# Eight x loads issued from ScalarE's queue in place of SyncE's in a fused state-space and mixer kernel

## The chip, the cores and the metric

The kernel runs on one core of one Trainium2 chip. The metric is the device time of one execution in microseconds. Three runs of the kernel before gave 232.43 us in the median (231.18 to 232.94).

The engines are named as in the profile: PE is TensorE, PEld its weight loads, DVE is VectorE, ACT is ScalarE, POOL is GpSimd, and SP is SyncE, which here issues DMAs and does nothing else. "SPq" in a profile line is SP's sequencer at work on an issue.

## The reference

Two blocks, one after the other, in float32. The first is a state-space block with decay, for 4 batches, 8 heads, 768 positions, head dimension 32 and state size 16, in chunks of positions:

```
cum = np.cumsum(log_a[chunk])                     # a clipped to [1e-6, 1]
M   = (C @ B.T) * exp(cum_i - cum_j) * causal
y   = M @ x + (C @ state) * exp(cum)
state = exp(sum(log_a)) * state + (B * exp(cum_last - cum)).T @ x
```

Its result, with the heads side by side as 256 columns, is `x` of the second block, a mixer:

```
h  = x.T @ U @ V                                  # over positions, rank 32
u  = x + h.T
out = u + relu(u @ w_ch1) @ w_ch2                 # 256 -> 1024 -> 256
```

U, V and the two w arrive as 64-bit floats and are turned into float32 on the chip, from their words.

## The kernel before, in words

**Tiling.** The 768 positions of a batch are three pairs of two blocks of 128; there are twelve pairs in all, numbered 0 to 11. For each pair there are five loads: `x` in two halves of 128 KB (`load_x`, lines 203 to 210), and B in two halves and C in one (`load_bc`, lines 188 to 201), which fill one `bc` tile. Tiles of `x` and of `bc` have four buffers each.

**Order.** The kernel is recorded under a manual schedule. Two strings of words give the whole order: `LOADS` (line 34) ahead of the constants, and `PLAN` (line 36) behind them. A word is a letter and numbers: `b2.0` is part 0 of the bc load of pair 2, `x2.0` is half 0 of its x load, `Z0` the four loads of V, `z0` the load of U, `W0` or `w5` a weight load, `c0` the next step in the conversion of a loaded weight. Each engine executes its instructions in the order in which the words record them. The words around the loads in question are

```
    'b0.0 b0.1 b0.2 x0.0 x0.1 b1.0 b1.1 b1.2 ')
    'b3.2 F1.1 F1.0 x1.1 x1.0 A0 Q0.1 Q0.0 Z0 A1 Q0.2 V0.1.1 V0.0.0 K0 s0 g0 m0 M0 n0 ...
    ... z0 c0 x2.1 c0 V2.1.3 n1 i1 c0 g2 m2 j1 y1 x2.0 s2 u2 ...
    ... j2 c1 y2 m3 x3.1 t1 O2.1 x3.0 c2 p0 b4.1 P4 s3 v0 ...
```

Behind `LOADS` stand the constants and the logarithm of the decays: the load of `a`, two transposes (line 329), a clip on VectorE, and `la` on ScalarE (line 335).

**The words.** `A0` and `A1` (`decays`) compute the decay factors `F`: products on TensorE, then an exponential on ScalarE (line 372). `Q` and `P` (`prep`) multiply the loaded B and C by `F` into `BC` on VectorE. `V` and `T` (`turn`) transpose `BC` on TensorE and copy the result to `T` and `Cm` on ScalarE or VectorE. `g` (`gram`, line 509) and `m`, `M` (`mask`) form the masked products of C and B. `s` (`state`, line 541) multiplies `BC` by `x`, and needs both halves of `x`; `u` (`update`) carries the state on, on VectorE. `n` (`intra`, line 633) multiplies the masked products by `x`; `i` and `j` (`inter`, line 611) add what comes from the state. `y` (`yout`, line 646) copies the result to `yT` on ScalarE. `t` and `O` transpose it to `ytok` (lines 654 and 663). `p`, `q`, `v`, `a` are the low-rank product of the mixer, `U`, `d`, `S`, `f`, `e`, `h` its two large products (line 726). `F` words are warm-up products on the identity (line 137).

**Queues.** All loads go through `begin` (line 183), which issues them from SP; results are stored from SP too (line 795). A load finished is told by a semaphore. There are eight of them for loads, given out in turn in the order of all loads, so that every load from the ninth on waits until the load eight places before it, on the same semaphore, has landed. A load into a buffer in use waits for the engine that reads it last. An instruction that waits holds up those behind it on its engine.

Of the kernel before, what the change touches and what calls it, by code (L numbers as in the profile page):

```python
# [13 lines left out]
FP32R = mybir.dt.float32r  # L14
WCOLS = 512
NWORDS = 15
PLAIN = 2
TAGS = {(2, 1): "yyy", (3, 0): "yyy", (3, 1): "yyy"}

# [56 lines left out]
def kernel(  # L76
# [27 lines left out]
    nc = tc.nc  # L104
# [42 lines left out]
    class Kept:  # L147
# [23 lines left out]
        out=a_sb,  # L171
# [3 lines left out]
    x_sb, bc_sb = {}, {}  # L175
    pairs = [(b, q) for b in range(NB) for q in range(NPR)]

    def hold(load, until):

        tc.add_manual_dep(load.ins, until.ins.name, mybir.DependencyInfo(  # L180
            mybir.DependencyClass.Sync, mybir.DependencyReason.DATA))

    def begin(**kwargs):
        op = nc.sync.dma_start(**kwargs)  # L184
        if until:
            hold(op, until.pop())

    def load_bc(k, parts=(0, 1, 2)):
        b, q = pairs[k]
        if k not in bc_sb:  # L190
            bc_sb[k] = raw.tile([P, NH, 2, 2, N], FP32, tag="bc", name="bc")
        for part in parts:
            if part == 1:
                begin(
                    out=bc_sb[k][:, :, 1].rearrange("p h t n -> p h (t n)"),
                    in_=C[b, :, ts(q, 2 * P), :].rearrange("h (p t) n -> p h (t n)", t=2))
            else:
                c = part // 2
                begin(
                    out=bc_sb[k][:, :, 0, c],  # L200
                    in_=B[b, :, ts(2 * q + c, P), :].rearrange("h s n -> s h n"))

    def load_x(k, blocks=(0, 1)):
        b, q = pairs[k]
        if k not in x_sb:
            x_sb[k] = raw.tile([P, 2, NH, D], FP32, tag="x", name="x")
        for c in blocks:
            begin(
                out=x_sb[k][:, c],
                in_=x[b, :, ts(2 * q + c, P), :].rearrange("h s d -> s h d"))  # L210


# [17 lines left out]
    def words_of(dst):  # L230
        p, i, j = dst.shape
        t = raw.tile([P, 2 * WCOLS], INT32, tag="words", name="words", bufs=NWORDS)
        weights.append((dst, t[:p, :2 * i * j]))
# [42 lines left out]
    def load(k):  # L276
        if k < NB * NPR:
            load_bc(k)
            load_x(k)

    loads = dict(B=load_bc, X=load_x, w=load_w, b=lambda k, p: load_bc(k, (p,)),
                 x=lambda k, c: load_x(k, (c,)), W=load_w, Z=lambda n: load_v(),
                 z=lambda n: load_u())
    for word in LOADS.split():
# [43 lines left out]
    for g in range(2):  # L328
# [3 lines left out]
        out=la.rearrange("p b c h -> p b h c"),  # L332
# [64 lines left out]
    def to_fp32(dst, words, n):  # L397
# [5 lines left out]
        def tmps(*dtypes):  # L403
            t = raw.tile([P, 2 * WCOLS], INT32, tag="words", name="words", bufs=NWORDS)
            return [t[:p, v * WCOLS:v * WCOLS + i * j].bitcast(d) for v, d in enumerate(dtypes)]
# [23 lines left out]
    def refine(c):  # L429
# [6 lines left out]
        yield  # L436
        far = raw.tile([P, 2 * WCOLS], INT32, tag="words", name="words", bufs=NWORDS).bitcast(
            FP32)[:, :WCOLS].rearrange("p (i j) -> p i j", i=near.shape[1])
# [232 lines left out]
    def mixer(b):  # L671
# [61 lines left out]
        def pair(dtype):  # L733
            t = raw.tile([P, 2 * WCOLS], INT32, tag="words", name="words", bufs=NWORDS)
            return t.bitcast(dtype)[:, :2 * HS].rearrange("p (m t) -> p m t", m=2)
# [35 lines left out]
        def down(j, k, n):  # L771

            parts = b or j >= PLAIN
            pieces = 6 if parts else 4
# [130 lines left out]
```

## Time and profile before

| | |
|---|---|
| median of three runs | 232.43 us |
| the profiled execution | 231.95 us |
| span of its profile | 230.2 us |
| TensorE busy | 219.4 us (95%) |
| VectorE busy | 158.5 us (69%) |
| ScalarE busy | 113.2 us (49%) |
| GpSimd busy | 14.3 us (6%) |
| x loads | 24, 128.0 KB each, 4.0 us from issue to landing in the median |
| chain that ended last | PE 82%, DVE 7%, DMA 5%, ACT 2%, issue 2%, SPq 1% |

The profile is of one execution. Its slices divide the span into forty; a digit is the busy share of an engine in tenths, and PEclk is the clock granted to TensorE in tenths of the full one. Timeline lines give start and duration in us, engine, line of the kernel, operation, output and input, shape and count, and in brackets how long the engine was idle just before and what ended that. Lines of the chain give start, duration and what ran or was waited for. A line of the DMA view gives destination and source, the issuing engine, the number of issues, KB of each and the median time from issue to landing. A line of busy time by stretch gives the stretch, its length, TensorE's busy time with the number of products, the granted clock, the share of the DMA engines and GB/s.

### The profile page before, as it was taken

Reading aid. Unit: us, or ns where it says so; the run is one execution under the profiler, and the core shown is the slowest. Engines: PE = TensorE matmul, PEld = TensorE weight load, DVE = VectorE, ACT = ScalarE, POOL = GpSimd, SP = SyncE. Lnnn points to the kernel's source line nnn. Section 1 sums busy time; section 2 is a strip of 40 time slices with the busy share of each in tenths; the row PEclk is TensorE's granted clock in tenths of the full one; section 3 lists DMA queues with packets and bytes.
Section 4 is the critical chain, followed back from the end, with each engine's and each line's share of the span. In section 5 each row is a group of like instructions: output and inputs, shape, how many; then the busy total and the mean of one; then the engine's idle time right before and its main releaser. Section 6 shows DMA issues by size and latency. Waiting matters only on the chain.

```text
span 230.2 us, 6970 instructions
## 1 busy us (share of the span) xinstructions
PE 219.4 (95%) x2994; PEld 182.6 (79%) x2994; DVE 158.5 (69%) x331; ACT 113.2 (49%) x260; POOL 14.3 (6%) x37
## 2 busy tenths in 40 slices
PE   7698899999999999999999999999999999999993
PEld 5444656656677898898799899798998899999993
DVE  4656879989998667657964766668725983765821
ACT  3334447866976247343523553466326526655510
POOL 3011201003100000110210000010000000000000
PEclk9977999999999999999999999999999999999999
DMA  6968796898826170001001035000001001000011
GB/s 90 117 98 146 129 228 146 248 164 157 114 34 89 29 111 23 23 4 48 3 7 41 1 62 107 21 3 1 3 23 48 0 0 48 6 17 26 24 46 46
DMA packets 69518, 14.56 MB, mean 63 GB/s; under 512 B 63792, under 2 KB 67696, under 8 KB 69488
## 3 DMA queue, kind: packets, MB, share of 16 engines
q1 hardware_dynamic: 69488, 14.13, 33.0%
q8 instruction: 23, 0.38, 0.7%
q14 instruction: 7, 0.06, 0.1%
HBM read 10.98 MB, written 3.15 MB: 61 GB/s over the span
## 4 chain that ended last, share of the span: by engine, by line
PE 82%; DVE 7%; DMA 5%; ACT 2%; issue 2%; SPq 1%; POOL 0%; DVEq 0%; ACTq 0%
PE x L726 28%; PE z L726 21%; PE y L726 12%; PE y L611 3%; PE y L633 3%; DMA x<-in_x_dram 3%; PE w L680 2%; PE x L509 2%; PE w L478 2%; PE w L654 2%; PE w L541 2%; DMA bc<-in_B_dram 2%; DVE S L158 1%; DVE words L158 1%; SPq L184 1%
## 5 line engine op out<-in xcount | busy, mean ns | idle before, releaser
L158 DVE SCALAR_TENSOR_TENSOR words<-words 128x768 fp32r<-128x768 f32 (+6 forms) x44 | 35.0, 814 | 1.1
L726 PE MATMUL x<-u,w 128*128 128x384 f32 x144 | 33.2, 350 | 0.0
L726 PE MATMUL z<-u,w 128*128 128x384 f32 x144 | 32.5, 344 | 0.0
L731 ACT ACTIVATE x<-x 128x384 f32<-128x384 f32 (+1 forms) x30 | 13.6, 454 | 29.7 <-PE x L726 29.6
L726 PEld LDWEIGHTS x<-u,w 128*128 128x128 f32 x144 | 24.2, 188 | 2.3 <-DVE words L158 0.8
L158 DVE SCALAR_TENSOR_TENSOR words<-x,words 128x384 fp32r<-128x384 f32 x24 | 13.3, 556 | 17.7 <-ACT words L760 16.9
L726 PEld LDWEIGHTS z<-u,w 128*128 128x128 f32 x144 | 24.4, 188 | 0.8 <-ACT z L731 0.4
L726 PE MATMUL x<-w2c,words 128*128 128x256 f32 x112 | 22.5, 341 | 0.0
L726 PEld LDWEIGHTS x<-w2c,words 128*128 128x128 f32 x112 | 18.2, 189 | 1.8 <-DVE w2c L158 0.3
L726 PE MATMUL y<-w,words 128*128 128x256 f32 x144 | 19.5, 282 | 0.0
L726 PEld LDWEIGHTS y<-w,words 128*128 128x128 f32 x144 | 18.7, 188 | 0.2
L731 ACT ACTIVATE z<-z 128x384 f32<-128x384 f32 (+1 forms) x27 | 12.5, 462 | 12.3 <-PE z L726 11.8
L158 DVE SCALAR_TENSOR_TENSOR words<-z,words 128x384 fp32r<-128x384 f32 x24 | 13.2, 550 | 3.3 <-ACT words L760 3.3
L760 ACT ACTIVATE words<-z 128x384 fp32r<-128x384 f32 x24 | 11.4, 490 | 6.7 <-PE z L726 6.7
L158 DVE SCALAR_TENSOR_TENSOR S<-S,kept,w 128x64 f32<-128x64 f32 x40 | 11.2, 279 | 4.3 <-PE w L541 2.4
L760 ACT ACTIVATE words<-x 128x384 fp32r<-128x384 f32 x24 | 11.5, 490 | 4.7 <-PE x L726 4.6
L567 POOL TENSOR_TENSOR Sm<-S,own 128x256 f32<-128x256 f32 (+1 forms) x12 | 8.9, 738 | 80.0 <-DVE S L158 74.9
L611 PE MATMUL y<-T,Sm 32*64 32x64 f32 x352 | 12.4, 240 | 1.2 <-POOL settled L574 0.9
L726 PE MATMUL x<-w,words 128*128 128x256 f32 x96 | 13.4, 287 | 0.0
L611 PEld LDWEIGHTS y<-T,Sm 32*64 32x64 f32 x352 | 8.7, 131 | 4.9 <-issue 2.0
L633 PEld LDWEIGHTS y<-M,x 64*32 64x32 f32 x768 | 8.9, 107 | 4.5 <-DVE M L158 1.2
L726 PEld LDWEIGHTS x<-w,words 128*128 128x128 f32 x96 | 12.1, 189 | 0.4
(147 smaller groups left out, 401.8 us busy)
## 6 DMA issues: line engine op xcount, KB each, us to landing
words<-in_moe_w_ch_dram SPq DMA_DIRECT2D x7, 512.0 KB, 6.5
x<-in_x_dram SPq DMA_DIRECT2D x24, 128.0 KB, 4.0
out_dram<-ytok SPq DMA_DIRECT2D x24, 128.0 KB, 1.7
bc<-in_B_dram SPq DMA_DIRECT2D x24, 64.0 KB, 3.6
bc<-in_C_dram SPq DMA_DIRECT2D x12, 128.0 KB, 3.4
words<-in_moe_w_ch_dram SPq DMA_DIRECT2D x2, 256.0 KB, 3.8
words<-in_moe_V_dram SPq DMA_DIRECT2D x4, 48.0 KB, 3.9
words<-in_moe_U_dram SPq DMA_DIRECT2D x1, 192.0 KB, 4.0
```

Of the source, the lines that this page charges most:

```text
L158: self.last = call(*args, **kwargs)
L478: nc.tensor.transpose(out=tp[:, i, v], in_=s["BC"][:, i, c + v].rearrange("p h n -> p (h n)"), identity=ident)
L509: nc.tensor.matmul(out=g[r][cols, c], lhsT=s["T"][rows, 0, c, cols], rhs=s["Cm"][rows, :, :, ts(2 * c + p, Q)].rearrange("r v t i -> r v i ...
L541: nc.tensor.matmul(out=s["A"][p][ts(r, Q), v], lhsT=s["BC"][half, 0, v, 2 * r:2 * r + 2].rearrange("p h n -> p (h n)"), rhs=x_sb[k][half, ...
L567: nc.gpsimd.tensor_tensor(out=s["Sm"][:, sl], in0=s["S"][:, sl].rearrange("p i (s d) -> p i s d", s=2), in1=own2[:, b, 4 * q + sl.start:4 ...
L611: product = nc.tensor.matmul(out=y[p][ts(r % 2, H), r // 2, c], lhsT=own[ts(r, Q)], rhs=s["T"][ts(r, Q), 1, :, ts(2 * c + p, Q)].rearrange ...
L633: product = nc.tensor.matmul(out=y[p][ts(i, Q), n, c], lhsT=x_sb[k][half, c, h], rhs=s["M"][half, h // 2, c, h % 2], start=fresh(k, p, [i] ...
L654: nc.tensor.transpose(out=t[:, c, g], in_=yT[b][:, g, ts(2 * q + c, P)], identity=ident)
L680: nc.tensor.matmul(out=p[ts(c % 4, Q)], lhsT=U_sb[:, c], rhs=ytok[b][:, c], start=c < 4, stop=True, skip_group_check=True)
L726: nc.tensor.matmul(out=t, lhsT=lhsT, rhs=rhs, start=start, stop=True, skip_group_check=True)
L731: nc.scalar.activation(t, t, AF.Copy, scale=1.0 + EPS)
L760: nc.scalar.activation(gs[j, m // 2][0][:, m % 2], t, AF.Relu, scale=NEAR)
```

## The change

`begin` takes the queue as an argument, SP's unless another is given. `load_x` gives it ScalarE's for pairs 0 to 3 (`k < OWN`), which are eight loads: x0.0, x0.1, x1.1, x1.0, x2.1, x2.0, x3.1 and x3.0. Neither `LOADS` nor `PLAN` changes. The loads of pairs 4 to 11, and all other loads and stores, stay on SP. The lines of the kernel behind the new constant move down by one, so that line 541 of before is line 542 of after.

```diff
+OWN = 4
...
-    def begin(**kwargs):
-        op = nc.sync.dma_start(**kwargs)
+    def begin(queue=nc.sync, **kwargs):
+        op = queue.dma_start(**kwargs)
         if until:
             hold(op, until.pop())
...
         for c in blocks:
             begin(
-                out=x_sb[k][:, c],
+                queue=nc.scalar if k < OWN else nc.sync, out=x_sb[k][:, c],
                 in_=x[b, :, ts(2 * q + c, P), :].rearrange("h s d -> s h d"))
```

## The prediction

> **What bounds the kernel now.** I read the slices first, then the chain of work that ended last, then the timelines of ScalarE, SP and TensorE around the moved loads. The slices (each a fortieth, 5.76 us):
>
> ```profile
> PE   7698899999999999999999999999999999999993
> ...
> PEclk9977999999999999999999999999999999999999
> DMA  6968796898826170001001035000001001000011
> ```
>
> TensorE is the bound, but its first five slices (to 29 us) have holes, and there the DMA engines are as full as anywhere. Busy time by stretch says the same: TensorE is busy for 28.22 of the first 34.10 us and for 151.16 of the last 155.20. The loads of the change lie among the holes; behind them little idle TensorE time is left that could take a delay back. The chain begins:
>
> ```profile
> 2.36 3.55 DMA bc<-in_B_dram
> ...
> 6.00 0.10 DVE BC L158
> ```
>
> The start hangs on a bc load of pair 0 until 6.00. From there to 39 us the chain goes through VectorE, TensorE and ScalarE by turns, with no x load in it: the x loads of pairs 0 to 3 are early. ScalarE, start and duration:
>
> ```profile
> 4.09 0.36 ACT L335 ACTIVATE la<-la 128x192 f32<-128x192 f32 x1 [2.00 <-DVE la L158]
> 5.36 0.34 ACT L372 ACTIVATE F<-w 128x192 f32<-128x192 f32 x1 [0.91 <-PE w L365]
> ...
> 24.45 0.65 ACT L646 COPY yT<-y 128x256 f32<-128x256 f32 x2 [1.19 <-PE y L611]
> ...
> 29.99 0.65 ACT L646 COPY yT<-y 128x256 f32<-128x256 f32 x2 [0.47 <-PE y L611]
> ```
>
> SP, with the first two x pairs and the V loads that matter below:
>
> ```profile
> 3.00 1.55 SPq L184 DMA_DIRECT2D x<-in_x_dram  x2
> ...
> 7.83 1.67 SPq L184 DMA_DIRECT2D x<-in_x_dram  x2
> 9.54 2.55 SPq L184 DMA_DIRECT2D words<-in_moe_V_dram  x4
> ```
>
> The same view has x of pair 2 at 15.58 (2.15) and of pair 3 at 22.89 (4.12). SP runs ahead of the work by much: TensorE takes up these two pairs at
>
> ```profile
> 24.31 0.43 PE L541 MATMUL w<-x,BC 64*32 64x64 f32 x24
> ...
> 32.74 0.32 PE L541 MATMUL w<-x,BC 64*32 64x64 f32 x8
> 33.27 0.43 PE L541 MATMUL w<-x,BC 64*32 64x64 f32 x24 [0.22 <-ACT pT L683]
> ```
>
> **The change, part by part.** Eight issues leave SP (1.55 + 1.67 + 2.15 + 4.12 = 9.49 us of its time) and stand in ScalarE's stream where the plan names them. No compute instruction changes its place on any engine. What changes is which work stands ahead of a load, and what a waiting load holds up. The changed program's order on ScalarE begins:
>
> ```
> 3 L336 Activation la<-la 128x192 [waits DVE_49]
> 4 L185 DMACopy x<-in_x_dram 128x8x32 [waits DMAHW3_49]
> 5 L185 DMACopy x<-in_x_dram 128x8x32 [waits DMAHW5_49]
> 6 L373 Activation F<-w 128x96x2 [waits PE_49] x2
> ```
>
> *Pair 0* waits for nothing and stands behind the table load (0.81 to 2.09). Two issues of 0.78 (half of 1.55) end by 3.7, ahead of la at 4.09: nothing. If they took longer, la would move by the excess, behind the larger wait that follows.
>
> *Pair 1* is the large term. Loads take eight completion semaphores in turn, and each waits for the load before it on its own. For x1.1 that is now the second V load, for x1.0 the fourth. On SP such a wait held up loads alone; on ScalarE it stands ahead of F, which everything needs. When does the fourth V load land? SP starts them at 9.54; without the two x pairs ahead (1.59 and 1.71 with their gaps) it starts at 6.24, and the fourth is issued three quarters of 2.55 later, at 8.15. The DMA view gives the time from issue to landing of these four, and of x4.0, issued to a quiet queue at 37.90:
>
> ```profile
> words<-in_moe_V_dram SPq DMA_DIRECT2D x4, 48.0 KB, 3.9
> ...
> x<-in_x_dram SPq DMA_DIRECT2D x1, 128.0 KB, 2.6
> ```
>
> 8.15 + 3.9 = 12.05. The traffic agrees: the last bc load ahead of the V loads is issued at 7.0 and lands 4.1 later, at 11.1, behind the same data. Then x1.0 is issued (0.78), and F starts at 12.9 in place of 5.36, 7.5 later. Of this 0.3 is covered: BC waits for its bc load until 6.00 though F ends at 5.70. **+7.2.** The ends: landing after 2.1 (the a load, into empty queues) gives +5.4; V landing no sooner than now (9.54 + 1.91 + 3.9 = 15.35) gives +10.5. Queued behind the wait are F on ScalarE, then BC on VectorE and the transposes on TensorE, so all engines shift together. x1 itself is issued by 12.9 and needed at 15.12 + 7.2: hidden.
>
> *Pair 2* (in the times of now; the shift is on both sides). x2.1 stands between two conversions of the U/V words (20.94, 21.38); its 0.78 fits into the 0.89 that ScalarE then idles ahead of 22.89; without that cover it costs 0.78. x2.0 stands behind the yT copies of pair 1, which end at 25.10, while the products need it at 24.31. Issue at 25.15, landing 2.6 later: TensorE takes it up at 27.8. **+3.5.** It takes work in order, and VectorE's state update (24.93) and BC behind it wait as well. With 4.7 us to landing (the median of the x loads before 52 us) it is +5.6; with the shortest of any bc load (2.3) +3.2. I take 2.6, since SP, rid of eight issues, should have its weight loads down by then.
>
> *Pair 3.* x3.1 is issued behind the yT copies of pair 2 (end 30.64), 0.5 of issue (0.99 for the quiet pair at 37.90), then the ytok copy (0.59), then x3.0 at 31.8. Landing at 34.4, against products whose last 24 start at 33.27 behind the first 8 (some 0.1): **+1.3.** With 4.7 it is +3.4; with 2.3, +1.0. The pT copy at 32.85 keeps its time, since ScalarE idles 1.38 ahead of it.
>
> *The eight issues off SP* bring bc and weight loads forward. VectorE's waits for bc after 6.00 are one of 0.54, off the chain; TensorE's one wait for an x load is 0.2. Nothing to gain, at most 0.7.
>
> *Clock.* Busy time by stretch shows half clock in windows of 3.4 us behind stretches of thin work:
>
> ```profile
> 11.80:15.20 3.40, 3.31 (x44) 0.50 0.51 73
> ```
>
> The window ahead of it has TensorE busy for 2.35 of 3.40 and full clock. Idling through 7.2 us can put the work now at 6 to 11.8 (about 2.4 us of TensorE on the chain) at half clock: up to +2.4; if the two half-clock windows of now then fall elsewhere, the warm products of 1.29 in each become 0.65: -1.3. I take the middle, **+0.5**. The Trainium skill, in "TensorE: Matmul & The Clock Gate", Part 1: The HAM clock gate, has the clock halved after one idle window of about 3.4 us; by that rule the upper end holds here, and the sum would be 1.9 higher. The row agrees in the length of its window.
>
> **Sum:** 7.2 + 3.5 + 1.3 + 0.5 = 12.5. The profiled execution took 231.95 us (span 230.2 and 1.7 around it), 0.5 under the median of 232.43. 231.95 + 12.5 = **244.5**.
>
> **The rivals.**
>
> 1. *The first stall alone.* While F waits, loads get ahead, and x2 and x3 might come in time. Against: both are named behind copies of the pair before, whatever the shift. 231.95 + 7.2 + 0.5 = 239.6.
>
> 2. *The late loads share the engines with the weights.* ScalarE's x2.0 and x3.0 then meet 512 KB loads: 4.7 to landing. For it: DMA digits of 7 to 9 until 58 us. 7.2 + 5.6 + 3.4 + 0.5 = 16.7: 248.7. With V late as well, 252.
>
> 3. *Faster: issuing binds.* SP's row is solid with issues up to 34 us; relieved, it brings each load earlier, and the waits for loads behind the start go: 0.3 ahead of BC, 0.54 and 0.2: 1.0, so 230.9. It decides if no ScalarE instruction is held, that is if the fourth V load lands before la ends at 4.45; that SP issues it at 11.45 now speaks against it. The Trainium skill, in "Perfetto Trace Analysis", DMA Optimizations, advises this very balancing when descriptor generation is the bottleneck; the chain, with SP in it for 1%, does not bear it out here.
>
> 4. *It does nothing:* ScalarE issues its loads past its waits, and the x loads are early enough: 232. Against: SP's own issues keep their order in every row.
>
> **How the numbers follow.** Forecast 0.62, rival 1 0.14, rival 2 0.19, rival 3 0.03, rival 4 0.02. The range is 239.5 to 250.0: below lie rivals 3 and 4, above the far end of rival 2 (V and x both late). About 1% is what a measurement of this kernel can tell from no change; slower by over 1% is 0.95, within it 0.03, faster 0.02 (rival 3 in part falls within).
>
> **What would show it.** In the changed profile F starts near 13, with ScalarE idle ahead of it and the V words as releaser; then waits of TensorE for x ahead of line 542, one near 32 us (some 3.5), one near 43 (some 1.3), and the chain with x loads in it there. From 46 us on everything should be the old profile, shifted. Wrong would be F near 6; TensorE without those two waits; or a tail that is not shifted, work having been caught up.

## The result and the profile after

The changed kernel takes 243.26 us in the median of four runs (242.08 to 244.36), the kernel before beside it 231.81 (230.31 to 232.94). The ratio is 1.050, with a 95% interval of 1.042 to 1.058: slower by 11.5 us, where 12.5 were forecast. The profiled execution took 243.45 us, with a span of 241.7 in place of 230.2: 11.5 by the profile too.

The slices of the changed kernel's page (a fortieth is now 6.04 us), its chain by engine, and its x loads on ScalarE:

```profile
PE   7077859798999999999999999999999999999994
...
PEclk9659967999999999999999999999999999999998
DMA  9898912088776516100100005300001001000011
...
PE 77%; DMA 10%; DVE 5%; SPq 4%; issue 2%; ACT 1%; ACTq 0%; POOL 0%; DVEq 0%
...
x<-in_x_dram ACTq DMA_DIRECT2D x8, 128.0 KB, 3.4
```

The zero in TensorE's row is new, and so is the 5 in the sixth slice. Behind the tenth slice the row is as full as before. DMA has 10% of the chain in place of 5%. ScalarE's timeline in the changed kernel shows where the zero comes from:

```profile
0.80 1.28 ACT L167 ACT_TABLE_LOAD   x1 [0.80 <-PEq L890]
0.84 1.10 ACTq L185 DMA_DIRECT2D x<-in_x_dram  x2
4.40 0.36 ACT L336 ACTIVATE la<-la 128x192 f32<-128x192 f32 x1 [2.32 <-DVE la L159]
11.64 1.01 ACTq L185 DMA_DIRECT2D x<-in_x_dram  x2
12.70 0.56 ACT L373 ACTIVATE F<-w 128x192 f32<-128x192 f32 x2 [7.93 <-DMA words<-in_moe_V_dram]
...
29.89 0.37 ACT L647 COPY yT<-y 128x256 f32<-128x256 f32 x1 [1.58 <-PE y L612]
29.90 0.37 ACTq L185 DMA_DIRECT2D x<-in_x_dram  x1
30.16 0.38 ACT L647 COPY yT<-y 128x256 f32<-128x256 f32 x1
...
40.20 0.59 ACT L664 COPY ytok<-w 128x512 f32<-128x512 f32 x1
40.21 0.45 ACTq L185 DMA_DIRECT2D x<-in_x_dram  x1
```

ScalarE idles 7.93 us ahead of F, until V has landed; the x loads of pair 1, which come ahead of F, are issued at 11.64. F starts at 12.70 in place of 5.36. By the trace x1.1 is issued when the second V load has landed (11.62), and x1.0 at 12.06, when the fourth has (12.01). The chain of the changed kernel has that wait, on the second V load, and two more, of which the kernel before has none:

```profile
8.24 3.38 DMA words<-in_moe_V_dram
...
29.90 2.85 DMA x<-in_x_dram
...
40.21 2.92 DMA x<-in_x_dram
```

And TensorE's timeline has the waits that answer to them, ahead of the state products of pairs 2 and 3:

```profile
32.79 0.65 PE L542 MATMUL w<-x,BC 64*32 64x64 f32 x24 [2.96 <-DMA x<-in_x_dram]
...
43.27 0.53 PE L542 MATMUL w<-x,BC 64*32 64x64 f32 x32 [0.80 <-DMA x<-in_x_dram]
```

How the delay builds up is best seen by taking the same VectorE instruction in two timelines: VectorE executes the same 331 instructions in the same order in each of these kernels. The table gives by how many us an instruction starts later than in the profile of the kernel before. The columns are the instruction's start in that profile: BC of pair 0 (6.00), the sum for kept (8.90), the state update of pair 1 (15.68), a mask of pair 2 just ahead of its state products (24.24), the state update behind them (25.40), a mask of pair 3 (30.41), a weight conversion behind the state products of pair 3 (34.95), and the last instruction (226.65).

| kernel | 6.00 | 8.90 | 15.68 | 24.24 | 25.40 | 30.41 | 34.95 | 226.65 |
|---|---|---|---|---|---|---|---|---|
| the change | 7.07 | 8.26 | 6.59 | 5.33 | 8.65 | 9.67 | 10.05 | 11.51 |
| only pair 0 | 1.54 | 1.54 | 1.57 | 1.55 | 1.54 | 1.53 | 1.53 | 1.00 |
| only pair 1 | 7.21 | 8.40 | 6.38 | 4.84 | 4.83 | 5.61 | 5.60 | 6.15 |
| only pair 2 | 0.35 | 1.54 | -0.20 | -1.45 | 4.59 | 5.65 | 5.63 | 6.23 |
| only pair 3 | 0.11 | 0.37 | -0.98 | 0.35 | 0.45 | 0.45 | 5.40 | 6.05 |
| pair 1, issued first | 1.34 | 2.53 | 0.51 | -1.04 | -1.04 | -1.05 | -0.96 | -0.58 |
| pairs 2 and 3, words moved ahead | 0.08 | 1.63 | -0.19 | -0.10 | -0.09 | -0.09 | -0.09 | 0.52 |
| all but pair 0 | 6.88 | 8.06 | 7.47 | 7.52 | 10.61 | 11.67 | 12.14 | 12.39 |
| all but pair 1 | 1.43 | 2.62 | 0.60 | -0.95 | 4.58 | 5.64 | 5.94 | 6.48 |
| the change, with fitted fills | 6.94 | 6.94 | 6.99 | 6.93 | 9.47 | 9.47 | 9.67 | 9.38 |

In the first row the delay is made in three places (ahead of 6.00, between 24.24 and 25.40, ahead of 34.95), and in between it shrinks by 1.74 and grows by 1.02. The experiments ask what each wait is due to, whether the parts add, and what moves the delay in between.

### The profile page after: what moved, and what is told of

Its sections match the earlier page's. It is cut to its first block, busy times and chain, and to the rows that moved or that the text cites. A ratio compares the mean times of both kernels' runs of the same rounds, so it can differ in the third digit from the quotient of the medians.

```text
span 241.7 us, 6969 instructions
## 1 busy us (share of the span) xinstructions
PE 220.6 (91%) x2994; PEld 184.8 (76%) x2994; DVE 159.3 (66%) x331; ACT 113.1 (47%) x260; POOL 14.3 (6%) x37
## 3 DMA queue, kind: packets, MB, share of 16 engines
q10 hardware_dynamic: 8320, 1.05, 2.9%
## 4 chain that ended last, share of the span: by engine, by line
PE 77%; DMA 10%; DVE 5%; SPq 4%; issue 2%; ACT 1%; ACTq 0%; POOL 0%; DVEq 0%
PE x L727 26%; PE z L727 19%; PE y L727 11%; DMA x<-in_x_dram 8%; PE y L634 4%; SPq L185 4%; PE y L612 3%; PE x L510 3%; PE w L479 2%; PE w L542 2%; PE w L655 2%; DMA words<-in_moe_V_dram 1%; DVE S L159 1%; PE w L681 1%; PE z L510 1%
## 5 line engine op out<-in xcount | busy, mean ns | idle before, releaser
L727 PEld LDWEIGHTS x<-u,w 128*128 128x128 f32 x144 | 24.2, 188 | 2.3 <-DVE words L159 0.8
L727 PEld LDWEIGHTS y<-w,words 128*128 128x128 f32 x144 | 18.6, 188 | 0.2
L732 ACT ACTIVATE z<-z 128x384 f32<-128x384 f32 (+1 forms) x27 | 12.5, 462 | 12.3 <-PE z L727 11.8
L159 DVE TENSOR_TENSOR BC<-bc,F 128x512 f32<-128x512 f32 (+2 forms) x18 | 9.2, 533 | 8.5 <-ACT F L373 8.0
L479 PE MATMUL w<-ident,BC 128*128 128x128 f32 x40 | 7.9, 313 | 7.5 <-DVE BC L159 7.5
L761 ACT ACTIVATE words<-x 128x384 fp32r<-128x384 f32 x24 | 11.5, 490 | 4.7 <-PE x L727 4.6
L612 PEld LDWEIGHTS y<-T,Sm 32*64 32x64 f32 x352 | 9.2, 135 | 5.4 <-issue 2.5
```

Source lines behind the costliest of these rows:

```text
L159: self.last = call(*args, **kwargs)
L479: nc.tensor.transpose(out=tp[:, i, v], in_=s["BC"][:, i, c + v].rearrange("p h n -> p (h n)"), identity=ident)
L612: product = nc.tensor.matmul(out=y[p][ts(r % 2, H), r // 2, c], lhsT=own[ts(r, Q)], rhs=s["T"][ts(r, Q), 1, :, ts(2 * c + p, Q)].rearrange ...
L727: nc.tensor.matmul(out=t, lhsT=lhsT, rhs=rhs, start=start, stop=True, skip_group_check=True)
L732: nc.scalar.activation(t, t, AF.Copy, scale=1.0 + EPS)
L761: nc.scalar.activation(gs[j, m // 2][0][:, m % 2], t, AF.Relu, scale=NEAR)
```

## The experiments

Each time is the median beside that of the kernel before, run on the same chip; the ratio stands with its interval and need not be the quotient of the two medians. There is one profile of each kernel; that of the kernel before is of an execution of 231.95 us. The theory: what costs is that each load stands in a stream that carries other work. A load that waits for its completion semaphore holds the compute instructions behind it, and a load behind compute instructions is late. The rivals: the second queue as such costs, by its issues in ScalarE's time or by contention; or the parts are independent and add.

### One pair at a time

```diff
-OWN = 4
+OWN = (0,)        # (1,), (2,) and (3,) in the other three
...
-                queue=nc.scalar if k < OWN else nc.sync, out=x_sb[k][:, c],
+                queue=nc.scalar if k in OWN else nc.sync, out=x_sb[k][:, c],
```

Pair 0:

> Pair 0 alone on ScalarE's queue; pairs 1 to 3 stay on SP. The prediction's step says: nothing, 0.0 us. Its rival, from the trace after: there x0 is issued at 0.84, in front of the last bc loads of pair 0, and the wait for F hides what that does. If the two x loads get ahead of bc on the DMA engines, the last bc load of pair 0 lands at about 7.4 in place of 5.9, and BC starts near 7.4 in place of 6.0: +1.4 us, of which the clock may give back or take some 0.5.

Measured: 233.04 beside 230.83, a ratio of 1.011 (1.005 to 1.018). The first BC in VectorE's timeline of this kernel:

```profile
7.54 0.83 DVE L159 TENSOR_TENSOR BC<-bc,F 128x128 f32<-128x128 f32 x3 [2.49 <-DMA bc<-in_B_dram]
```

It starts 1.54 later than in the kernel before and waits 2.49 for bc, where it waited 1.25. The x loads, issued at 0.83 in place of 3.00, are ahead of the bc loads on the DMA engines, and every column of the table but the last (1.00) keeps the 1.5. The prediction's "nothing" is wrong for this pair by itself.

Pair 1:

> Pair 1 alone on ScalarE's queue. x1.1 waits on the semaphore of the second bc load ahead of V, x1.0 on that of the second V load. If the wait on the semaphore holds F, F starts at 12 to 13.5 in place of 5.4, and of this shift of 7 some 1.7 is given back by 24 us, since the half-clock windows fall elsewhere: +5 to +7 us at the end. If the issue itself is what holds F (its own duration, a busy queue), F is late by 1 to 1.5 us alone and the end by as much.

Measured: 239.09 beside 230.83, 1.035 (1.030 to 1.039): 8.3 us, above the 5 to 7 expected; the profiled execution, the shortest of its four, is 6.2 later by its span. The longest wait of ScalarE in the first 20 us of this kernel (engine and line, releaser, us in total, times, longest):

```profile
ACT F L373 <- DMA words<-in_moe_V_dram: 8.5, 1, 8.5
```

Pair 2:

> Pair 2 alone on ScalarE's queue. If late issue is the cause, x2.0 is issued when the second yT copy of pair 1 has been released (24.5), lands 2.9 later in a quiet queue, TensorE takes it up at 27.4 in place of 24.3, and half-clock windows behind the stall add 1: +4 us. SP is less relieved than in the whole change, so x2.0 may meet weight loads: 4.7 to landing, then +6. If late issue alone is no matter and x2 only suffered from the first shift, 0.

Measured: 238.00 beside 230.83, 1.029 (1.025 to 1.033): 7.2 us. TensorE's wait for x in this kernel:

```profile
28.73 0.65 PE L542 MATMUL w<-x,BC 64*32 64x64 f32 x24 [5.80 <-DMA x<-in_x_dram]
```

x2.0 is issued at 24.45, though the copies ahead of it start at 23.00: it also waits for x2.1, with which it shares a semaphore here, and which lands 4.2 after its issue at 20.20. x2.0 takes another 4.2.

Pair 3:

> Pair 3 alone on ScalarE's queue. x3.0 is issued at 30.6. In a quiet queue it lands 2.9 later, at 33.5, and TensorE loses 0.4 us, as in the whole change. Here, however, SP issues its 512 KB weight loads at 28 to 34 us, which in the whole change were long down: if the two queues share the DMA engines, x3.0 takes 4.7 to 7 us and costs +2 to +4. By the first +0.4, by the second +2 to +4; nothing if lateness is no matter.

Measured: 237.35 beside 230.83, 1.027 (1.022 to 1.030): 6.5 us. In the DMA view x3.0, issued at 31.00, takes

```profile
x<-in_x_dram ACTq DMA_DIRECT2D x1, 128.0 KB, 7.3
```

and TensorE waits for it:

```profile
38.42 0.68 PE L542 MATMUL w<-x,BC 64*32 64x64 f32 x32 [5.17 <-DMA x<-in_x_dram]
```

In this kernel SP issues a 512 KB load at 29.43, which takes 8.4, so that the two queues bring their data at once. In the whole change the same x3.0 takes 2.92, on engines with nothing else to do. The Trainium skill has it so: "DMA: Bandwidth & Descriptors", Issuing engines are not separate DMA queues, says that loads from different engines run on the same sixteen DMA engines and interleave. The 7.3 beside 2.92 agrees.

Alone, the four cost 1.0, 6.2, 6.2 and 6.1 us by their spans, 19.5 together (by the medians 2.2, 8.3, 7.2 and 6.5, 24.2 together). The whole change costs 11.5. They do not add.

### What holds F: the wait, or the issue

```diff
-    'b0.0 b0.1 b0.2 x0.0 x0.1 b1.0 b1.1 b1.2 ')
+    'b0.0 b0.1 b0.2 x1.1 x1.0 x0.0 x0.1 b1.0 b1.1 b1.2 ')
...
-    'b3.2 F1.1 F1.0 x1.1 x1.0 A0 Q0.1 Q0.0 Z0 A1 Q0.2 ...
+    'b3.2 F1.1 F1.0 A0 Q0.1 Q0.0 Z0 A1 Q0.2 ...
```

with `OWN = (1,)`.

> Pair 1 alone on ScalarE's queue, as in only1, but its two loads are moved ahead of the x loads of pair 0 in LOADS, so that they are among the first eight loads and wait on no semaphore. If the wait behind the V loads is what held F, F starts at 5.5 to 5.9, and what is left is the cost of two x loads ahead of the bc loads of pair 0, as in only0: BC at 7.5, +1.5 us at the end. If it is the second queue or the issue on ScalarE as such, F is late as in only1: +5 us or more.

Measured: 232.74 beside 231.77, 1.006 (1.002 to 1.010): 7 us less than with the same two loads at their old place. ScalarE's timeline:

```profile
0.83 1.10 ACTq L185 DMA_DIRECT2D x<-in_x_dram  x2
4.34 0.36 ACT L336 ACTIVATE la<-la 128x192 f32<-128x192 f32 x1 [2.26 <-DVE la L159]
5.80 0.34 ACT L373 ACTIVATE F<-w 128x192 f32<-128x192 f32 x1 [1.10 <-PE w L366]
```

F is at 5.80. So it is the wait behind the V loads that held it, not the queue; of the issues, the 0.59 us of x1.0 behind that wait (12.06 to 12.65 in the changed kernel) have a share. BC comes 1.34 late, as with pair 0 alone; this execution then gains 3.6 us by 24 us (table). That goes with the clock, below: the page records no half-clock window for this kernel, where the kernel before has two.

```profile
PEclk9999999999999999999999999999999999999999
```

### Late, or on the wrong queue

```diff
-... V1.0.2 F3.1 Q1.1 V1.1.2 u0 s1 ... b2.1 y0 Q2.0 m1 ... c0 x2.1 c0 ... y1 x2.0 s2 ... m3 x3.1 t1 O2.1 x3.0 c2 ...
+... V1.0.2 F3.1 Q1.1 V1.1.2 x2.1 x2.0 u0 s1 ... b2.1 y0 x3.1 x3.0 Q2.0 m1 ... c0 c0 ... y1 s2 ... m3 t1 O2.1 c2 ...
```

with `OWN = (2, 3)`.

> Pairs 2 and 3 on ScalarE's queue, with their words moved ahead in the plan: x2 ahead of u0 s1, x3 ahead of Q2.0 m1, some 8 to 12 us sooner than where they stand. If lateness is what costs, no TensorE wait for x is left, and the time is that of the kernel before within 0.7 us. If the second queue as such costs (shared engines, issues in ScalarE's stream), +2 us or more.

Measured: 232.47 beside 231.77, 1.006 (1.002 to 1.010). TensorE has no wait for x at either place, and takes the state products of pairs 2 and 3 up within 0.1 us of where the kernel before does:

```profile
24.21 0.43 PE L542 MATMUL w<-x,BC 64*32 64x64 f32 x24
...
32.65 0.32 PE L542 MATMUL w<-x,BC 64*32 64x64 f32 x8
```

So ScalarE's queue carries these four loads at a cost of 0.6% (0.2 to 1.0), if they are issued 8 us or more ahead of their use (x2.1 at 15.13, x3.1 at 18.41). Lateness is what costs. Nor is there a gain: SP, rid of them, brings nothing forward that was waited for.

### Do the parts hide each other

All but pair 0 (`OWN = (1, 2, 3)`):

> Pairs 1 to 3 on ScalarE's queue, pair 0 back on SP. If the wait of F hides what the x loads of pair 0 cost (+1.5 alone, in only0), taking them out changes nothing: F near 12.7 and the time of the changed kernel within 0.7 us. If the costs add, 1.5 to 2 us less than the changed kernel.

Measured: 242.23 beside 231.77, 1.051 (1.045 to 1.057), against 1.050 for the whole change. By the medians it is 1.0 us below the changed kernel (243.26), so that the times leave anything from 0 to 1 us for pair 0. By the trace most of its 1.5 us is hidden: F starts at

```profile
12.50 0.56 ACT L373 ACTIVATE F<-w 128x192 f32<-128x192 f32 x2 [8.04 <-DMA words<-in_moe_V_dram]
```

in place of 12.70, and BC is 6.88 late in place of 7.07.

All but pair 1 (`OWN = (0, 2, 3)`):

> Pairs 0, 2 and 3 on ScalarE's queue as in the change, pair 1 on SP. Alone, pairs 0, 2 and 3 cost 1.0, 6.2 and 6.1 us by their profiles. If the costs add, +13. If a wait for one pair lets the loads behind it run ahead, the wait for x2 (about 5) gives SP the time to bring its weight loads down, x3.0 then meets a quiet queue and lands some 3 us after its issue in place of 7.3, and TensorE loses 0.5 to 1 on it in place of 5.2: +7 to +8 in all.

Measured: 238.22 beside 231.94, 1.026 (1.018 to 1.034): some 6 us, less than pair 2 alone in its runs, and less than half of the 13.3 that the three cost alone by their spans. TensorE's waits for x are

```profile
28.70 0.65 PE L542 MATMUL w<-x,BC 64*32 64x64 f32 x24 [5.27 <-DMA x<-in_x_dram]
...
39.16 0.46 PE L542 MATMUL w<-x,BC 64*32 64x64 f32 x32 [0.68 <-DMA x<-in_x_dram]
```

and x3.0, issued at 36.22, takes

```profile
x<-in_x_dram ACTq DMA_DIRECT2D x1, 128.0 KB, 2.8
```

SP issues its last 512 KB load ahead of x4 at 25.99 and has nothing further on the way by then. The first wait in the row thus pays for a part of the later ones: loads on SP run ahead while the engines stand, and the next late load meets idle DMA engines. In the whole change the wait ahead of F plays this part for pair 2 as well (2.85 to landing in place of 4.2).

### The clock

```diff
-    ... Z0 A1 Q0.2 V0.1.1 ...     ... j1 y1 x2.0 s2 ...
+    ... Z0 A1 F40.2 Q0.2 V0.1.1 ...     ... j1 y1 x2.0 F16.3 s2 ...
```

The added `F` words are warm-up products on the identity; their results are not used.

> The changed kernel with warm-up products of no use to the result in TensorE's two long waits: ten of 128x512 behind the decay products, four ahead of the state products of pair 2. If half clock behind the waits has a price, the clock stays full in the first wait, the shift at the state update of pair 0 is 7.1 in place of 8.3, and behind the second wait 8.7 in place of 9.7: 1 to 2 us less than the changed kernel. If the waits alone set the time, it is that of the changed kernel (243.3 beside 231.8 for before).

Measured: 245.62 beside 231.77, 1.064 (1.057 to 1.070), 2.4 us above the changed kernel. It told nothing of the clock, since a 128x512 warm-up product was longer than I had reckoned (8.85 us for ten): the fills ended behind what they were to bridge. With sizes that fit, `F28.2` and `F8.3`:

> As the run warm, with fills that end before what is waited for: in warm a 128x512 warm-up product took 0.89 us at full clock, and both fills ran past the loads by 1.4 to 1.6 us. Seven of them here (6.2 us from 6.2) and two (1.8). If half clock behind the waits has a price of its own, this is 0.5 to 1.5 us below the changed kernel, with the state update of pair 0 later by 7.1 to 7.5 in place of 8.3; if what counts is only where the half-clock windows of the kernel before and of this one fall, the shift by 24 us stays near 7 in place of 5.3, and the time is that of the changed kernel or 1 us above it.

Measured: 241.24 beside 231.94, 1.040 (1.035 to 1.045), against 1.050 (1.042 to 1.058): some 2 us less than the changed kernel, 2.1 by the spans (239.6 and 241.7), more than the 0.5 to 1.5 expected. The intervals overlap; the executions (239.74 to 241.85 and 242.08 to 244.36) do not. Busy time by stretch of the changed kernel (stretch, length, TensorE's busy time, then of PEld, VectorE, ScalarE and GpSimd, granted clock, DMA share, GB/s):

```profile
8.40:18.60 10.20, 4.84 (x74) 3.64 (x74) 2.74 (x8) 1.98 (x7) 0.33 (x1) 0.50 1.07 155
18.60:32.30 13.70, 9.67 (x294) 6.28 (x294) 9.89 (x31) 5.30 (x16) 1.67 (x4) 1.00 0.87 185
32.30:39.10 6.80, 6.31 (x146) 4.75 (x150) 2.83 (x8) 2.63 (x6) 1.07 (x2) 0.50 0.02 4
```

and of the kernel with fitted fills:

```profile
5.20:18.80 13.60, 11.15 (x134) 5.76 (x132) 3.95 (x12) 1.98 (x7) 0.33 (x1) 1.00 1.30 150
18.90:22.30 3.40, 3.34 (x56) 1.69 (x64) 1.57 (x7) 1.05 (x4) 0.62 (x1) 0.50 0.77 91
22.30:25.70 3.40, 2.30 (x89) 1.58 (x74) 2.86 (x9) 0.98 (x4) 0.81 (x2) 1.00 0.98 245
25.70:29.10 3.40, 3.34 (x16) 1.37 (x22) 1.31 (x5) 2.25 (x7) 0.00 (x0) 0.50 1.09 301
```

With the fills the half-clock windows lie where those of the kernel before lie, 7.1 us later (before: 11.8 to 15.2 and 18.6 to 22.1), and the table's last row has a delay that stays at 6.9 from 6.00 to 24.24. Without them the clock is half from 8.4 to 18.6, and the delay rises to 8.26; then it is full for four windows, in two of which the kernel before has half, and the delay falls to 5.33. Behind the second wait, half clock from 32.3 to 39.1 adds 1.02 in the change (8.65 to 9.67), and nothing with the fills (9.47 and 9.47).

By the two profiles, however, most of the 2 us is not this price. With the fills the first wait gives nothing back (6.93 at 24.24 in place of 5.33). The second then costs 2.54 in place of 3.32, with x2.0 landing 0.5 sooner behind its issue (2.34 in place of 2.85), and the 1.02 behind it are saved. At 34.95 the two kernels are 0.38 us apart. The other 1.75 arise behind that, where the clock is full in both: there TensorE waits 1.1 us for x loads in the changed kernel (at 59.2, 59.8 and 67.2), and not at all with the fills.

The Trainium skill, "TensorE: Matmul & The Clock Gate", Part 1: The HAM clock gate, has windows of 3.4 us and half clock behind an idle one. The traces agree in the length, and with pair 1 alone in the rest: TensorE does nothing there from 6.5 to 9.9, and the clock is half from 9.9 on. But the window ahead of half clock need not be idle: TensorE is busy for 0.96 us of the one from 5.0 to 8.4 in the changed kernel, and for 2.35 of the 3.40 from 8.4 to 11.8 in the kernel before, and in each the clock is half from the window's end on.

## Why the prediction was right, and where not

**Pair 1, +7.2: right in mechanism and sum, with luck in its inputs.** The forecast had the fourth V load landing at 12.05, F at 12.9 and a delay of 7.2. Measured: landed at 12.01, x1.0's wait and issue over at 12.65, F at 12.70, BC 7.07 late. Pair 1 alone gives 7.21, and the same loads without the wait 1.34. The one choice that mattered, V's landing from SP's issue without the two x pairs, came out to 0.04 us because two errors of 1 us made up for each other: SP issued the fourth V load at 9.17, not at 8.15, and it landed 2.84 behind that, not 3.9. (I had also taken the four V issues of the kernel before as equally long; the fourth begins there at 11.67, not 11.45.)

**Pair 0, nothing: right in the whole, wrong by itself.** I asked whether its issues delay ScalarE. They don't, but its data delay the bc loads: +1.5 alone. In the whole change the wait for F covers all but 0.2 of this, as F's start in "all but pair 0" shows.

**Pair 2, +3.5: right within 0.2.** The step between 24.24 and 25.40 is 3.32, TensorE's wait 2.96. Both inputs were off and in part made up for each other: x2.0 is issued with the start of the first yT copy, not behind the end of the second (0.6 sooner), and lands after 2.85 in place of 2.6. That SP's weight loads would be down by then nearly held: the last of them lands at 31.74, a microsecond ahead of x2.0. Without the wait for F it would not have held (4.2). And x2.1, which I had charged with its issue alone, is issued beside these weight loads at 26.21 and lands at 32.26, only 0.5 ahead of x2.0.

**Pair 3, +1.3: too large.** The step is 0.38, TensorE's wait 0.80. The term that was mis-sized is the time of issue: I stacked up the yT copies, x3.1's issue and the ytok copy ahead of x3.0 by their ends, and had it 1.2 us behind the ytok copy's place in the kernel before. It was issued as soon as that copy had begun.

**Clock, +0.5: wrong in sign, and not only in size.** I priced the half clock behind the wait and took its ends from the kernel before, but did not see that the full clock comes back later just where the kernel before has its half-clock windows. The half clock behind the first wait cost 1.19 up to 8.90 (7.07 to 8.26), half of the 2.4 that I gave as its upper end, and more than that came back. The first wait gained 1.74 by this in all, the second lost 1.02: together -0.7. With fills that keep the clock where it was both are gone, so the price is there; it is the difference of two patterns, each that of one execution. By 34.95 the fills are worth 0.4 us; the rest of their 2 us belongs to the next paragraph.

**What is left: +1.5 between 34.95 and the end.** The forecast was a tail that only shifts. From 35 to 49 us it does (10.05 and 10.06), then it grows by 1.2 us up to 72, in steps at waits for loads; a further 0.3 comes near 147. In the kernel with all but pair 1 the delay grows by 0.5 behind 34.95, near 147 too; in the one with fills it falls by 0.3. TensorE's waits for x loads between 48 and 90 us are 1.1 in the changed kernel, 0.2 in the kernel before and none with the fills. I did not test why these loads are late; the cause stays open, and it may be this one execution's.

The terms as measured, 7.07 - 1.74 + 3.32 + 1.02 + 0.38 + 1.46, make 11.51. The forecast of 12.5 came near because it was 0.9 too high on pair 3, 1.2 too high on the clock and 0.3 on pairs 1 and 2, and 1.5 too low on the tail.

**The rivals.** The first stall alone would have given 239.6; the waits ahead of line 542 exclude it. Sharing with the weights, 248.7, decides with pair 3 alone (7.3 to landing). In the whole change it happens to x2.1 (6.0 to landing), but x2.0, issued later, lands later still, and x3.0 meets no weight load. (The DMA digits that I gave for this rival are 6 to 9 up to 58 us, not 7 to 9.) That issuing binds, so that the change is faster: against it stand the loads of pairs 2 and 3 moved ahead, which take four of SP's issues away without any wait and gain nothing. The Trainium skill's advice in "Perfetto Trace Analysis", DMA Optimizations, to balance issues over engines has its condition, that descriptor generation be the bottleneck, and no run here met it.

No version that I tried beats the kernel before. The nearest are the two at 1.006.

## What to carry to other kernels

A DMA that is moved from a queue of its own into a compute engine's stream takes its semaphore wait along, and everything behind it on that engine then waits too: ask of each moved load which earlier transfer its semaphore belongs to and what compute stands behind it. Ask also when that engine will reach it, since a stream that executes compute in order cannot run ahead as an idle queue does. Costs of such waits are not to be added up: the first lets other loads run ahead and pays for the next, and a part that is free in the whole may not be free alone.

## What the runs showed of the hardware

- ScalarE's sequencer issues a DMA while the instructions ahead of it still execute: two x loads at 0.84, with the table load running from 0.80 to 2.08; x2.0 at 29.90, between two copies that both stand ahead of it in the order and start at 29.89 and 30.16.
- The half-clock windows, 3.4 us long, do not begin at a fixed time of the kernel. The first recorded change is one to full clock, and falls at 5.0, 6.6 and 11.3 in the executions of three kernels with the same first 5 us of TensorE work (before, only pair 0, only pair 2). Ahead of it a 128x128 product takes 421 ns, behind it 273; the PEclk row counts that stretch as full all the same. Where they fall moved the delay of a kernel by up to 3.6 us within its first 24 (pair 1 issued first: 2.53 to -1.04).
- An x load of 128 KB on ScalarE's queue takes 2.3 to 2.9 us with little or nothing else on the way (2.34 with the fills, 2.8 in all but pair 1, 2.92 in the change), 4.2 beside bc and x loads, and 6.0 and 7.3 beside 512 KB loads on SP's (x2.1 in the change, x3.0 with pair 3 alone).
